# Hash attention and SwiGLU on one core: another order of loads, and two more head pairs turned by TensorE

## The chip, the core and the metric

The kernel runs on one core of one Trainium2 chip. The metric is device time in microseconds of one execution. Three runs of the kernel before gave 378.98, 381.4 and 386.73 us (median 381.4). A separate execution was profiled; it took 378.15 us, and its span from the first to the last instruction is 376.4 us.

## The reference

Four batches, eight heads, 768 tokens, 64 values per head. Every token of q and k gets a bucket of six bits, the signs of its products with a 64 x 6 matrix. A query attends only to keys of its own bucket. The attention output is laid out as 3072 rows of 512 and goes through RMS norm and a SwiGLU network without bias.

```
q_bits = (einsum('bhsd,dk->bhsk', q, proj) > 0);  k_bits likewise
mask   = bucket(q_bits)[..., :, None] == bucket(k_bits)[..., None, :]
scores = where(mask, q @ k^T / 8, -1e9);  attn = softmax(scores);  o = attn @ v
x  = o as [B*S, H*D];  xn = x / sqrt(mean(x*x) + 1e-6) * rms_g
y  = (silu(xn @ w_gate) * (xn @ w_val)) @ w_out        # d_ff = 1536
```

## The kernel before, in words

**Mask by extra rows.** The mask is not applied to the scores. Beside the 64 values, the transposed q and k in tile `QK` have 12 more rows with scaled bits, so that the product q.k over 76 rows (`KROWS`) is pulled far down wherever the bits differ. These rows come from `hash_head` (one head), `hash_heads` (a pair) or `hash_two` (two pairs): products of the transposed fp32 q and k with `proj` on TensorE (`hash_bank`, L202), a comparison on DVE (`signs`, L209), and copies of 12 rows to partitions 64 to 75 of `QK`. [...]

**Turning.** q and k arrive with tokens on partitions and must be transposed. Batch 0 is turned by TensorE per head (`turn_head`, `turn_pe`, L155): three 128 x 128 transposes for k and three for q into a PSUM bank, copied to fp32 tiles `kT` (DVE, L162) and `qT` (ACT, L165), cast to `QK` by ACT and POOL. A bank of PSUM comes from pool `gps`, three in all, which also serves the hash, the gate, value and output products. A `QK` half of a batch 0 head has four blocks of 384 columns: t = 0 even chunks of k, 1 even chunks of q, 2 odd chunks of k, 3 odd chunks of q. Batches 1 to 3 are loaded in blocks of 32 tokens (`load_blocks`: eight DMAs of 96 KB for a pair, 128-byte runs) and turned on DVE by 32 x 32 transposes (`turn_dve`, L186: four instructions for a pair), then cast on POOL (`cast_pool`, L194).

**Units, slots and steps.** A unit is a half batch (384 queries, all 8 heads); the first half of batch 0 is cut in two (units 0 and 1 with 128 and 256 queries). Every head of a unit has one to three slots; a slot is one 128 x 768 tile of scores. There are 192 slots, and the main loop has a step for each: it issues the scores of slot s+1 (L324), the exponential of slot s on ACT (L334), and then everything that `plan[s]` holds, in the order in which `at(s, ...)` was called. Unit 0 has steps 0 to 7, unit 1 steps 8 to 23, each later unit 24 steps from `BASE` (24, 48, 72, ...). `plan` thus is an order written by hand on every engine. It holds: AV products of a head one to three steps later (L348); normalisation (`attn_out`, `norm`); the FFN of the unit before, one gate (L434), one value product (L445) and two DVE operations (L447, L448) at a time; the output products (`project`, L459, from step 23) and their store on SP (L468); loads, turns and hashes of coming heads (table `spots`); and the weight loads.

**Queues.** SP's queue takes loads, bit transfers and stores in the order of the steps; an entry that waits holds up those behind it. POOL issues the weight loads (`load_w` wg and wv in halves at steps 1, 3, 5, 7; `load_wo` at steps 12 and 15), which also cast fp32 to fp16. Raw loads of q, k and v go through pool `lpool` of eight buffers: a new load waits until the tile eight places before it is free. The loads of batch 0 are issued ahead of the loop up to pair 1's v; those of pair 3 at step 1, the last two v at steps 2 and 3.

**Start.** Eight products of zeros (L505, 128 x 512) keep TensorE busy until the first load lands; then heads 0 and 1 are turned, both are hashed, and the scores of slot 0 follow.

Of the kernel before, what the change touches and what calls it, by code (L numbers as in the profile page):

```python
# [36 lines left out]

@with_exitstack
def kernel(
# [16 lines left out]
    lpool = ctx.enter_context(tc.tile_pool(name="lpool", bufs=8))  # L56
# [15 lines left out]
    zeros16 = const.tile([128, 512], FP16, name="zeros16")  # L72
# [20 lines left out]
    def raw_tile(b, hp, which):  # L93
        shape = [128, 24, 32] if b and which != "v" else [128, 2, 6, D]
        raw[b, hp, which] = lpool.tile(shape, FP32, name=which + "L", tag="L")
        return raw[b, hp, which]
# [25 lines left out]

    T0, QK = {}, {}

    def qk_tile(b, hp):
        QK[b, hp] = qkpool.tile([128, 2, 2 * S], FP16, name="QK")
# [6 lines left out]
    def t0(hp, which, hh):  # L133
        return T0[0, hp, which][:, hh * HALF : (hh + 1) * HALF]

    def koff(b, jt):
        return (jt // 3) * S + (jt % 3) * 128 if b == 0 else S + jt * 128

    def qoff(w):
        b, half = divmod(w, 2)  # L140
        return half * S + HALF if b == 0 else half * HALF

    def vchunk(b, jt):
        return 2 * (jt % 3) + jt // 3 if b == 0 else jt

    def turn_pe(h, which):
        hp, hh = divmod(h, 2)
        if (0, hp) not in QK:
            qk_tile(0, hp)
        if hh == 0:  # L150
            t_tile(0, hp, which)
        src = raw[0, hp, which][:, hh].rearrange("p (c e) d -> p c (e d)", e=2)
        ps = bank("t_ps", [128, 3, 128])
        for i in range(3):
            nc.tensor.transpose(ps[:, i, :], src[:, i], ident)  # L155
        return ps.rearrange("p c t -> p (c t)")

    def block(h, t):
        return QK[0, h // 2][0:64, h % 2, t * HALF : (t + 1) * HALF]

    def keep_k(h, ps):
        nc.vector.tensor_copy(t0(h // 2, "k", h % 2), ps)  # L162

    def keep_q(h, ps):
        nc.scalar.copy(t0(h // 2, "q", h % 2), ps)  # L165
        nc.scalar.copy(block(h, 1), ps[0:64])

    def cast_pool0(h, which, par):
        src = t0(h // 2, which, h % 2)[64 * par : 64 * par + 64]
        nc.gpsimd.tensor_copy(block(h, 2 * par + (which == "q")), src)  # L170

    def turn_head(h):
        keep_k(h, turn_pe(h, "k"))
        keep_q(h, turn_pe(h, "q"))
        cast_pool0(h, "k", 0)
        cast_pool0(h, "k", 1)

    def turn_dve(b, hp, which, part):
        if (b, hp) not in QK:
            qk_tile(b, hp)  # L180
# [33 lines left out]
    def bit_rows(h, t):  # L214
        return QK[0, h // 2][D:KROWS, h % 2, t * HALF : (t + 1) * HALF]

    def hash_head(h, q_by_act=False):
        hp, hh = divmod(h, 2)
        kt, qt = t0(hp, "k", hh), t0(hp, "q", hh)
        ps = hash_bank([(pk[:, 0:32], kt), (pq[:, 0:32], qt), (pk[:, 12:44], kt)])  # L220
        bt = spool.tile([128, S], FP16, name="bits")
        signs(bt[:, 0:HALF], ps, 96)
        if q_by_act:
            nc.scalar.copy(bit_rows(h, 1), bt[32:44, 0:HALF])
        nc.vector.tensor_copy(bit_rows(h, 0), bt[0:12, 0:HALF])
        if not q_by_act:
            nc.vector.tensor_copy(bit_rows(h, 1), bt[32:44, 0:HALF])
        nc.vector.tensor_copy(bit_rows(h, 2), bt[64:76, 0:HALF])
        return bt

    def late_bits(h, bt):
        nc.sync.dma_start(out=bit_rows(h, 3), in_=bt[44:56, 0:HALF])

    def hash_heads(hp):
        ps = hash_bank(
            [(w, t0(hp, which, hh)) for hh in range(2) for w, which in ((pk, "k"), (pq, "q"))
             for w in (w[:, 0:32],)]
        )
        bt = spool.tile([128, S], FP16, name="bits")
        signs(bt[:, 0:HALF], ps)  # L240
        for hh in range(2):
            nc.sync.dma_start(
                out=bit_rows(2 * hp + hh, 2), in_=bt[64 * hh + 12 : 64 * hh + 24, 0:HALF]
            )
        for hh in range(2):
            for t in range(2):
                p0 = 64 * hh + 32 * t
                nc.vector.tensor_copy(bit_rows(2 * hp + hh, t), bt[p0 : p0 + 12, 0:HALF])
        for hh in range(2):
            nc.sync.dma_start(  # L250
                out=bit_rows(2 * hp + hh, 3), in_=bt[64 * hh + 44 : 64 * hh + 56, 0:HALF]
            )
# [63 lines left out]
    def scores(g):  # L316
        u, h, p = SLOTS[g]
        w, c0, n = UNITS[u]
        b = w // 2
        t = QK[b, h // 2][0:KROWS, h % 2]  # L320
        ps = scps.tile([128, 2, 512], FP32, name="s_ps")
        for jt, i0, ni, bk, col in score_parts(n, p):
            ko, qo = koff(b, jt), qoff(w) + 128 * c0 + i0
            nc.tensor.matmul(  # L324
                ps[:, bk, col : col + ni], t[:, ko : ko + 128], t[:, qo : qo + ni],
                start=True, stop=True,
            )
        sps[g] = ps
# [9 lines left out]
    def av(u, h, i0, i1):  # L338
        w, c0, n = UNITS[u]
        b = w // 2  # L340
        hp, hh = divmod(h, 2)
        if hh == 0 and i0 == 0:
            ot[u, hp] = ops.tile([128, 3, 2, 66], FP32, name="o_ps")
        o = ot[u, hp]
        for i in range(i0, i1):
            c, jt = divmod(i, 6)
            p, bk, col = prob_at(n, jt, c)
            nc.tensor.matmul(  # L348
                o[:, c, hh, 0:65],
                psb[u, h][:, p, bk, col : col + 128],  # L350
                vls[b % 2][:, h, vchunk(b, jt), 0:65],
                start=(hh == 0 and i == 0), stop=(jt == 5),
                skip_group_check=True,
            )
# [99 lines left out]
    def project(w, c, f0, f1):  # L454
# [8 lines left out]
        if f1 == NF:  # L463
# [4 lines left out]
            nc.sync.dma_start(out=rows[:, 2 * c + half if b == 0 else 3 * half + c, :], in_=ysb)  # L468
# [14 lines left out]
    load_rows(nc.sync, 0, 1, "v")  # L483

    nc.vector.memset(zeros16, 0.0)
# [14 lines left out]
    nc.vector.memset(ones16, 1.0)  # L500
# [3 lines left out]
    for i in range(8):  # L504
        nc.tensor.matmul(wz, zeros16[:, 0:128], zeros16, start=True, stop=True)  # L505
# [27 lines left out]
    turn_head(0)  # L533
    turn_head(1)
    bt0 = hash_head(0, q_by_act=True)
    bt1 = hash_head(1)
# [8 lines left out]
    at(0, late_bits, 0, bt0)  # L545
    at(0, late_bits, 1, bt1)
# [10 lines left out]
    at(3, hash_heads, 3)  # L557
    at(4, v_prep, 0, 2)
    at(1, load_rows, nc.sync, 0, 3, "k")
    at(1, load_rows, nc.sync, 0, 3, "q")  # L560
    at(2, load_rows, nc.sync, 0, 2, "v")
    at(3, load_rows, nc.sync, 0, 3, "v")
    at(5, lambda: nc.sync.dma_start(out=gcol, in_=moe_rms_g.rearrange("(k p) -> p k", p=128)))
    at(6, v_prep, 0, 3)
    for h in range(H):
        at(8 + h, cast_pool0, h, "q", 1)
# [7 lines left out]
    spots = {  # L574
# [3 lines left out]
    }  # L578
    for b, (loads, turns) in spots.items():
        for hp in range(4):  # L580
            s = loads[hp]
            at(s, load_blocks, nc.sync, b, hp)
            at(s, load_rows, nc.sync, b, hp, "v")
            s = turns[hp]
            at(s, turn_dve, b, hp, "k", 0)
            at(s + 1, turn_dve, b, hp, "k", 1)
            at(s + 2, cast_pool, b, hp, "k")
            at(s + 2, turn_dve, b, hp, "q", 0)
            at(s + 3, turn_dve, b, hp, "q", 1)
            at(s + 4, cast_pool, b, hp, "q")  # L590
            if hp % 2:
                at(s + 5, hash_two, b, hp - 1)
            at(s + 5, v_prep, b, hp)
            if b > 1:
                at(s + 5, v_sum, b, hp)
                if hp % 2:
                    at(48 * b + 1 + hp, v_mean, b, hp - 1, 4)
            else:
                at(48 * b + 5 + hp, v_mean, b, hp, 2, range(6))
# [107 lines left out]
```

## Time and profile before

| what | us |
|---|---|
| profiled execution | 378.15 |
| its span | 376.4 |
| median of three runs (lowest, highest) | 381.4 (378.98, 386.73) |
| TensorE busy | 337.9 (90%) |
| DVE, ACT, POOL busy | 238.9, 207.6, 136.6 |
| exponential, L334: 192 of 0.811 | 148.3 |
| DVE transposes, L186: 48 of 0.87 | 41.4 |
| weight loads: time to landing | 7.1 to 11.2 each |

The profile lists for each line of the kernel what ran, how long, and what ended the idle time in front of it. PE is TensorE's products, PEld its weight loads, SPq and POOLq the instructions that issue DMAs. The granted clock of TensorE is given in tenths in the page and as a fraction in the table by stage. `t_ps` are the transposes by TensorE, `d_ps` the hash products, `s_ps` the scores, `o_ps` AV, `g_ps` and `v_ps` gate and value, `y_ps` the output; `kL`, `qL`, `vL` the raw loads.

### The profile page before, as it was taken

The numbers are of one execution on the slowest core, as the hardware profiler recorded it, in microseconds if no ns is written. First come the engines' busy times: TensorE is split into PE (matmuls) and PEld (weight loads), VectorE is DVE, ScalarE is ACT, GpSimd is POOL, SyncE is SP. The second block draws the span as 40 slices with busy tenths as digits, with TensorE's granted clock in tenths as the row PEclk, the third lists the DMA queues.
The fourth block names the chain that finished last, engine by engine and source line by source line (L and its number), as shares of the span: only waits on it lengthen the run. The fifth ranks groups of instructions, "written<-read, shape, count | busy, mean of one in ns | idle before, by whom it ended". The sixth has DMA issues, their size and how long they took to land.

```text
span 376.4 us, 8018 instructions
## 1 busy us (share of the span) xinstructions
PE 337.9 (90%) x3088; PEld 210.2 (56%) x3088; DVE 238.9 (63%) x554; ACT 207.6 (55%) x342; POOL 136.6 (36%) x209
## 2 busy tenths in 40 slices
PE   7627698798979999999999999999999999998995
PEld 3415586476546565565556555656556655664552
DVE  3625256498956895698469846886566636575670
ACT  3414477575635674566656565775566755661331
POOL 4325472066741474286028711773111111111000
PEclk9987689999999999999999999999999999999999
DMA  7273999955074991100589701000100010002002
GB/s 238 101 150 85 215 187 202 170 106 110 14 156 89 151 158 54 73 2 8 91 165 217 128 17 57 29 2 16 57 30 0 2 57 28 2 3 75 12 0 84
DMA packets 91174, 31.42 MB, mean 83 GB/s; under 512 B 77592, under 2 KB 88064, under 8 KB 91136
## 3 DMA queue, kind: packets, MB, share of 16 engines
q1 hardware_dynamic: 87088, 25.80, 31.0%
q0 software_dynamic: 3680, 4.72, 8.0%
q8 instruction: 24, 0.39, 0.5%
q10 hardware_dynamic: 368, 0.39, 0.3%
q14 instruction: 14, 0.11, 0.1%
HBM read 28.32 MB, written 6.29 MB: 92 GB/s over the span
## 4 chain that ended last, share of the span: by engine, by line
PE 73%; DVE 10%; DMA 8%; ACT 3%; issue 2%; SPq 2%; POOL 1%; DVEq 0%; POOLq 0%; ACTq 0%
PE g_ps L434 15%; PE y_ps L459 15%; PE s_ps L324 14%; PE v_ps L445 14%; PE o_ps L348 8%; PE d_ps L202 3%; DMA wo<-in_moe_w_out_dram 3%; DMA qL<-in_q_dram 2%; DMA QK<-bits 2%; DVE xnT L418 2%; DVE kT L186 2%; ACT psb L334 2%; DMA kL<-in_k_dram 1%; DVE bits L209 1%; PE x_ps L417 1%
## 5 line engine op out<-in xcount | busy, mean ns | idle before, releaser
L334 ACT ACTIVATE psb<-s_ps 128x768 f16<-128x768 f32 x192 | 148.3, 811 | 10.7 <-PE s_ps L324 10.6
L324 PE MATMUL s_ps<-QK 76*128 76x384 f16 (+2 forms) x448 | 96.8, 310 | 12.0 <-DMA QK<-bits 4.9
L436 ACT ACTIVATE t<-g_ps 128x384 f32<-128x384 f32 (+2 forms) x108 | 49.2, 456 | 72.0 <-PE g_ps L434 68.8
L445 PE MATMUL v_ps<-xnT,wv 128*128 128x384 f16 (+2 forms) x432 | 80.5, 309 | 3.0 <-DVE a L447 2.8
L434 PE MATMUL g_ps<-xnT,wg 128*128 128x384 f16 (+2 forms) x432 | 80.5, 309 | 1.9 <-DVE xnT L418 1.7
L459 PE MATMUL y_ps<-wo,ht 128*128 128x512 f16 x288 | 70.6, 378 | 1.5 <-DMA wo<-in_moe_w_out_dram 1.5
L447 DVE SCALAR_TENSOR_TENSOR a<-t,g_ps 128x384 f32<-128x384 f32 (+2 forms) x108 | 54.1, 501 | 27.4 <-ACT t L436 26.5
L324 PEld LDWEIGHTS <-QK 76*128 76x128 f16 x448 | 42.5, 101 | 43.6 <-issue 13.8
L348 PEld LDWEIGHTS <-psb 128*128 128x128 f16 x1152 | 53.9, 99 | 18.9 <-issue 3.7
L448 DVE SCALAR_TENSOR_TENSOR ht<-a,v_ps 128x384 f16<-128x384 f32 (+2 forms) x108 | 55.1, 510 | 13.4 <-PE v_ps L445 3.1
L348 PE MATMUL o_ps<-vl,psb 128*128 128x65 f16 x1152 | 59.5, 195 | 0.4 <-ACT psb L334 0.2
L372 POOL TENSOR_TENSOR x<-otmp,rcp 128x384 f32<-128x384 f32 (+2 forms) x27 | 20.4, 756 | 105.1 <-DVE rcp L369 105.0
L445 PEld LDWEIGHTS <-wv 128*128 128x128 f16 x432 | 38.3, 98 | 22.8 <-issue 4.6
L434 PEld LDWEIGHTS <-wg 128*128 128x128 f16 x432 | 38.7, 98 | 21.3 <-issue 2.5
L466 ACT COPY ysb<-y_ps 128x512 f32<-128x512 f32 x24 | 14.1, 586 | 61.0 <-PE y_ps L459 57.8
L459 PEld LDWEIGHTS <-ht 128*128 128x128 f16 x288 | 25.8, 97 | 26.6 <-issue 2.4
L364 DVE TENSOR_TENSOR otmp<-o_ps,cvb 128x390 f32<-128x390 f32 (+2 forms) x36 | 18.5, 513 | 17.3 <-PE o_ps L348 17.2
L194 POOL CAST QK<-qT 64x768 f16<-64x768 f32 x24 | 19.7, 822 | 12.3 <-DVE qT L186 11.5
L418 DVE TENSOR_TENSOR xnT<-x_ps,gcol 128x512 f16<-128x512 f16 x24 | 15.2, 685 | 13.6 <-PE x_ps L417 13.5
L400 POOL TENSOR_SCALAR ms<-ss 128x3 f32<-128x3 f32 (+2 forms) x9 | 1.8, 195 | 56.6 <-DVE ss L398 56.6
L384 POOL TENSOR_TENSOR sq<-x 128x384 f32<-128x384 f32 (+2 forms) x27 | 20.4, 755 | 2.1
L194 POOL CAST QK<-kT 64x768 f16<-64x768 f32 x24 | 19.9, 829 | 3.1 <-DVE kT L186 1.7
(68 smaller groups left out, 261.2 us busy)
## 6 DMA issues: line engine op xcount, KB each, us to landing
vL<-in_v_dram SPq DMA_DIRECT2D x16, 384.0 KB
out_dram<-ysb SPq DMA_DIRECT2D x24, 256.0 KB
qL<-in_q_dram SPq DMA_DIRECT2D x48, 96.0 KB
kL<-in_k_dram SPq DMA_DIRECT2D x48, 96.0 KB
wg<-in_moe_w_gate_dram POOLq DMA_DIRECT2D x2, 768.0 KB, 8.2
wv<-in_moe_w_val_dram POOLq DMA_DIRECT2D x2, 768.0 KB, 7.9
wo<-in_moe_w_out_dram POOLq DMA_DIRECT2D x2, 768.0 KB, 10.4
kL<-in_k_dram SPq DMA_DIRECT2D x3, 384.0 KB
```

Source lines behind the costliest of these rows:

```text
L194: nc.gpsimd.tensor_copy(QK[b, hp][0:64, hh, o : o + S], T0[b, hp, which][64 * hh : 64 * hh + 64, :])
L324: nc.tensor.matmul(ps[:, bk, col : col + ni], t[:, ko : ko + 128], t[:, qo : qo + ni], start=True, stop=True,)
L334: nc.scalar.activation(psb[u, h][:, p], sps.pop(g)[:, :, 0:HALF], AF.Exp, scale=ESCALE,)
L348: nc.tensor.matmul(o[:, c, hh, 0:65], psb[u, h][:, p, bk, col : col + 128], vls[b % 2][:, h, vchunk(b, jt), 0:65], start=(hh == 0 and i == ...
L372: eng.tensor_mul(xd.rearrange("p c (h d) -> p c h d", h=2), tmp[:, 0:n, :, 0:64], r[:, 0:n].to_broadcast([128, n, 2, 64]),)
L418: nc.vector.tensor_mul(xnT[w][:, :, c * 128 : (c + 1) * 128], ps, gcol.unsqueeze(2).to_broadcast([128, 4, 128]),)
L434: nc.tensor.matmul(g, wg[:, kt, fs], xnT[w][:, kt, cs], start=(kt == 0), stop=(kt == 3))
L436: nc.scalar.activation(t, g, AF.Tanh, scale=0.5)
L445: nc.tensor.matmul(vv, wv[:, kt, fs], xnT[w][:, kt, cs], start=(kt == 0), stop=(kt == 3))
L447: nc.vector.scalar_tensor_tensor(out=a, in0=t, scalar=1.0, in1=g, op0=ALU.add, op1=ALU.mult)
L448: nc.vector.scalar_tensor_tensor(out=ht[w][:, ft, cs], in0=a, scalar=0.5, in1=vv, op0=ALU.mult, op1=ALU.mult)
L459: nc.tensor.matmul(y, ht[w][:, ft, c * 128 : (c + 1) * 128], wo[:, ft, :], start=(ft == 0), stop=(ft == NF - 1),)
```

## The change

- **Start.** The warm-up has 28 products of 128 columns in place of eight of 512, with ones in place of zeros. Head 0 is hashed before head 1 is turned. In `hash_head` ACT always copies the q bits.
- **Loads of batch 0.** `lpool` has ten buffers. Pair 1's v, then pair 3's k and q are issued at step 0 right behind pair 1's first bit transfers; the last two v at step 1. The bits of block 3 (odd q, used only from the second half of the batch on) leave `hash_heads`; `late_bits` sends them on SP at steps 3 and 5 to 7.
- **Batch 1, pairs 0 and 1** are in `BY_PE`: loaded in rows (three DMAs of 384 KB a pair, at steps 8 and 12), turned by TensorE, a head's k or q per step at steps 10 to 13 and 16 to 19, copied by DVE (k) and ACT (q), cast on POOL in two halves a step later, and hashed a pair at a time at steps 14 and 20, with all four bit blocks by DMA on SP. `k_cols`, `q_cols`, `v_chunk` and `out_chunk` hold the layouts of chunks; batch 1 now stores even and odd chunks, and for its pairs 2 and 3, still turned by DVE, the score's queries are read with a stride between chunks.
- **Other turns.** The four transposes of a pair stand two steps apart, in table `work`, where before all four stood in consecutive steps. Loads, hash and v of a pair move with them: loads eight steps before the turn (nine in two cases), the v one step after q and k, hash and v preparation two steps after the last transpose. `load_wo` is at steps 9 and 11.

The core of the diff:

```diff
-    lpool = ctx.enter_context(tc.tile_pool(name="lpool", bufs=8))
+    lpool = ctx.enter_context(tc.tile_pool(name="lpool", bufs=10))
+BY_PE = [(0, hp) for hp in range(4)] + [(1, 0), (1, 1)]
...
+    def q_cols(w, h, i0, ni):
...
+        if b == 1:
+            return t[:, 0:S].rearrange("p (c e t) -> p e c t", e=2, t=128)[:, half]
...
+    def keep(eng, b, h, which):
+        ps = turn_pe(b, h, which)
+        (eng.copy if eng is nc.scalar else eng.tensor_copy)(t0(b, h, which), ps)
+        return ps
...
+    def hash_heads(b, hp):
+        ps = hash_bank(
+            [(w[:, 0:32], t0(b, 2 * hp + hh, which))
+             for hh in range(2) for w, which in ((pk, "k"), (pq, "q"))]
+        )
+        bt = bits_tile(hp + 1 if b == 0 else hp)
+        signs(bt, ps)
         for hh in range(2):
+            h, p0 = 2 * hp + hh, 64 * hh
+            nc.sync.dma_start(out=bit_rows(b, h, 2), in_=bt[p0 + 12 : p0 + 24])
+            if b == 0:
+                for t in range(2):
+                    nc.vector.tensor_copy(bit_rows(b, h, t), bt[p0 + 32 * t : p0 + 32 * t + 12])
+                late[h] = bt[p0 + 44 : p0 + 56]
+            else:
+                for t in range(2):
+                    nc.sync.dma_start(
+                        out=bit_rows(b, h, t), in_=bt[p0 + 32 * t : p0 + 32 * t + 12]
+                    )
+                nc.sync.dma_start(out=bit_rows(b, h, 3), in_=bt[p0 + 44 : p0 + 56])
...
-    load_rows(nc.sync, 0, 1, "v")
...
-    for i in range(8):
-        nc.tensor.matmul(wz, zeros16[:, 0:128], zeros16, start=True, stop=True)
+    for i in range(28):
+        nc.tensor.matmul(wz[:, 0:128], ones16, ones16, start=True, stop=True)
...
     turn_head(0)
+    hash_head(0)
     turn_head(1)
-    bt0 = hash_head(0, q_by_act=True)
-    bt1 = hash_head(1)
+    hash_head(1)
     scores(0)
...
-    at(0, hash_heads, 1)
+    at(0, hash_heads, 0, 1)
+    at(0, load_rows, nc.sync, 0, 1, "v")
+    at(0, load_rows, nc.sync, 0, 3, "k")
+    at(0, load_rows, nc.sync, 0, 3, "q")
     at(0, turn_head, 4)
     at(1, turn_head, 5)
-    at(1, hash_heads, 2)
+    at(1, hash_heads, 0, 2)
+    at(1, load_rows, nc.sync, 0, 2, "v")
+    at(1, load_rows, nc.sync, 0, 3, "v")
...
+    at(3, late_bits, 0)
+    at(3, late_bits, 1)
...
-    at(1, load_rows, nc.sync, 0, 3, "k")
-    at(1, load_rows, nc.sync, 0, 3, "q")
-    at(2, load_rows, nc.sync, 0, 2, "v")
-    at(3, load_rows, nc.sync, 0, 3, "v")
+    for h in range(2, H):
+        at(4 + h // 2, late_bits, h)
...
-        at(12 + 3 * i, load_wo, 6 * i, 6 * i + 6)
-
-    spots = {
-        1: ((16, 20, 33, 38), (32, 37, 43, 48)),
-        2: ((52, 56, 63, 68), (61, 67, 80, 86)),
-        3: ((96, 100, 106, 112), (104, 110, 128, 134)),
+        at(9 + 2 * i, load_wo, 6 * i, 6 * i + 6)
+    work = {
+        (1, 0): (8, (10, 11, 12, 13)), (1, 1): (12, (16, 17, 18, 19)),
+        (1, 2): (25, (33, 35, 37, 39)), (1, 3): (33, (41, 43, 45, 47)),
+        (2, 0): (50, (58, 60, 62, 64)), (2, 1): (58, (66, 68, 70, 72)),
+        (2, 2): (74, (82, 84, 86, 88)), (2, 3): (81, (89, 91, 93, 95)),
+        (3, 0): (97, (105, 107, 109, 111)), (3, 1): (105, (113, 115, 117, 119)),
+        (3, 2): (121, (130, 132, 134, 136)), (3, 3): (129, (137, 139, 141, 143)),
     }
+    for (b, hp), (s, turns) in work.items():
+        done = turns[3] + 2
+        if (b, hp) in BY_PE:
+            at(s, load_rows, nc.sync, b, hp, "k")
+            at(s, load_rows, nc.sync, b, hp, "q")
+            at(s + 1, load_rows, nc.sync, b, hp, "v")
+            for i, s in enumerate(turns):
+                h, which = 2 * hp + i // 2, "kq"[i % 2]
+                at(s, keep, nc.scalar if i % 2 else nc.vector, b, h, which)
+                for par in range(2):
+                    at(s + 1, cast_half, b, h, which, par)
+            at(turns[3] + 1, hash_heads, b, hp)
```

More of the change, by code (lines that the diff above doesn't have):

```diff
@@ L93, in raw_tile @@
     def raw_tile(b, hp, which):
-        shape = [128, 24, 32] if b and which != "v" else [128, 2, 6, D]
+        shape = [128, 24, 32] if which != "v" and (b, hp) not in BY_PE else [128, 2, 6, D]
         raw[b, hp, which] = lpool.tile(shape, FP32, name=which + "L", tag="L")
@@ L125, in qk_tile @@
     def qk_tile(b, hp):
-        QK[b, hp] = qkpool.tile([128, 2, 2 * S], FP16, name="QK")
+        if (b, hp) not in QK:
+            QK[b, hp] = qkpool.tile([128, 2, 2 * S], FP16, name="QK")
     def t_tile(b, hp, which):
@@ L212, in signs @@
         )
[L214 to L219, printed above, removed]
-        ps = hash_bank([(pk[:, 0:32], kt), (pq[:, 0:32], qt), (pk[:, 12:44], kt)])
[L221 to L229, printed above, removed]
@@ L231, in late_bits, with bit_rows, bits_tile, hash_head @@
-    def late_bits(h, bt):
-        nc.sync.dma_start(out=bit_rows(h, 3), in_=bt[44:56, 0:HALF])
-    def hash_heads(hp):
+    def bit_rows(b, h, t):
+        return QK[b, h // 2][D:KROWS, h % 2, t * HALF : (t + 1) * HALF]
+    late = {}
+    held = []
+    def bits_tile(i):
+        if i % 2 == 0:
+            held.append(spool.tile([128, S], FP16, name="bits"))
+        return held[-1][:, (i % 2) * HALF : (i % 2 + 1) * HALF]
+    def hash_head(h):
+        kt, qt = t0(0, h, "k"), t0(0, h, "q")
+        ps = hash_bank([(pk[:, 0:32], kt), (pq[:, 0:32], qt), (pk[:, 12:44], kt)])
+        bt = bits_tile(h)
+        signs(bt, ps, 96)
+        nc.scalar.copy(bit_rows(0, h, 1), bt[32:44])
+        nc.vector.tensor_copy(bit_rows(0, h, 0), bt[0:12])
+        nc.vector.tensor_copy(bit_rows(0, h, 2), bt[64:76])
+        late[h] = bt[44:56]
@@ L235, in hash_heads, with late_bits @@
+    def late_bits(h):
+        nc.sync.dma_start(out=bit_rows(0, h, 3), in_=late[h])
+    def hash_heads(b, hp):
         ps = hash_bank(
-            [(w, t0(hp, which, hh)) for hh in range(2) for w, which in ((pk, "k"), (pq, "q"))
-             for w in (w[:, 0:32],)]
-        )
-        bt = spool.tile([128, S], FP16, name="bits")
-        signs(bt[:, 0:HALF], ps)
+            [(w[:, 0:32], t0(b, 2 * hp + hh, which))
+             for hh in range(2) for w, which in ((pk, "k"), (pq, "q"))]
+        )
+        bt = bits_tile(hp + 1 if b == 0 else hp)
+        signs(bt, ps)
@@ L241, in hash_heads @@
         for hh in range(2):
[L242 to L252, printed above, removed]
+            h, p0 = 2 * hp + hh, 64 * hh
@@ L467, in project @@
             rows = out[b * S : (b + 1) * S, :].rearrange("(p c) n -> p c n", c=6)
-            nc.sync.dma_start(out=rows[:, 2 * c + half if b == 0 else 3 * half + c, :], in_=ysb)
+            nc.sync.dma_start(out=rows[:, out_chunk(w, c), :], in_=ysb)
             del obank[w, c]
@@ L571 @@
         at(s1, load_w, wv, moe_w_val, 768 * i, 768 * i + 768)
-        at(12 + 3 * i, load_wo, 6 * i, 6 * i + 6)
-    spots = {
[3 rows of a table removed]
-    }
-    for b, (loads, turns) in spots.items():
-        for hp in range(4):
-            s = loads[hp]
-            at(s, load_blocks, nc.sync, b, hp)
[L583 to L590, printed above, removed]
-            if hp % 2:
[L592 to L599, printed above, removed]
+        at(9 + 2 * i, load_wo, 6 * i, 6 * i + 6)
+    work = {
[6 rows of a table added]
+    }
+    for (b, hp), (s, turns) in work.items():
[10 more added lines that the diff above has]
+            at(turns[3] + 1, hash_heads, b, hp)
+        else:
+            at(s, load_blocks, nc.sync, b, hp)
+            at(s + 1, load_rows, nc.sync, b, hp, "v")
+            for i, s in enumerate(turns):
+                at(s, turn_dve, b, hp, "kq"[i // 2], i % 2)
+                if i % 2:
+                    at(s + 1, cast_pool, b, hp, "kq"[i // 2])
+            if hp % 2:
+                at(done, hash_two, b, hp - 1)
+        at(done, v_prep, b, hp)
+        if b == 1:
+            at(48 + 2 * hp, v_mean, b, hp, 2, range(6))
+        else:
+            at(done, v_sum, b, hp)
+            if hp % 2:
+                at(48 * b + 1 + hp, v_mean, b, hp - 1, 4)
     gts, sqs = {}, {}
```

76 lines of the change are left out of this document (36 added, 40 removed).

## The prediction

> **What bounds the kernel now.** I read the page first, then busy time by stage, then what TensorE waited for up to 62 us, then the order of time on TensorE, SP and POOL around those waits.
>
> ```profile
> span 376.4 us, 8018 instructions
> PE 337.9 (90%) x3088; PEld 210.2 (56%) x3088; DVE 238.9 (63%) x554; ACT 207.6 (55%) x342; POOL 136.6 (36%) x209
> PEclk9987689999999999999999999999999999999999
> ```
>
> TensorE is busy 90% of the span, so 38.5 us are idle, and the clock falls only at the start. The table by stage (PE, PEld, DVE, ACT, POOL busy, granted clock, DMA share, GB/s) says where:
>
> ```profile
> 10.00:20.00 10.00, 7.21 (x58) 4.48 (x58) 5.82 (x14) 5.31 (x12) 4.52 (x9) 1.00 0.21 75
> 20.00:30.00 10.00, 2.17 (x20) 1.38 (x18) 2.09 (x6) 0.53 (x1) 1.27 (x2) 0.78 0.86 200
> 30.00:40.00 10.00, 5.88 (x62) 4.38 (x60) 4.61 (x14) 3.92 (x7) 6.80 (x12) 0.84 0.45 66
> 40.00:50.00 10.00, 8.41 (x95) 7.46 (x96) 3.98 (x14) 6.21 (x8) 5.45 (x11) 0.67 1.20 210
> ...
> 62.20:98.20 36.00, 30.05 (x335) 21.10 (x334) 26.51 (x62) 23.30 (x40) 15.59 (x21) 1.00 0.66 125
> 98.20:142.15 43.95, 40.82 (x388) 24.23 (x385) 34.09 (x71) 25.46 (x40) 23.50 (x31) 1.00 0.71 124
> 142.15:182.00 39.85, 39.05 (x353) 23.12 (x354) 29.07 (x61) 23.58 (x38) 20.18 (x28) 1.00 0.09 28
> ```
>
> From 20 to 50 us TensorE works 16.5 us of 30, part of it at half clock. From 142 us it is busy 39.05 of 39.85 us for 24 steps: there only less TensorE work saves time. Between, 62 to 142 us, 9 us are idle. The waits up to 62 us, and the lines around them (start, length, in brackets the idle time before):
>
> ```profile
> PE t_ps L155 <- DMA kL<-in_k_dram: 8.8, 2, 7.7
> PE s_ps L324 <- DMA QK<-bits: 4.9, 2, 4.1
> ```
>
> ```profile
> 17.95 0.33 PE L324 MATMUL s_ps<-QK 76*128 76x128 f16 x3 [0.83 <-DMA QK<-bits]
> 20.46 0.50 PE L324 MATMUL s_ps<-QK 76*128 76x128 f16 x6
> 28.62 0.87 PE L155 MATMUL t_ps<-ident,kL 128*128 128x128 f32 x3 [7.65 <-DMA kL<-in_k_dram]
> 31.33 0.83 PE L324 MATMUL s_ps<-QK 76*128 76x128 f16 x6
> 40.66 0.50 PE L324 MATMUL s_ps<-QK 76*128 76x128 f16 x3 [4.08 <-DMA QK<-bits]
> ```
>
> ```profile
> 15.97 1.48 SPq L242 DMA_DIRECT2D QK<-bits  x2
> 21.08 1.48 SPq L242 DMA_DIRECT2D QK<-bits  x2
> 24.19 0.46 SPq L106 DMA_DIRECT2D kL<-in_k_dram  x1
> 35.13 1.53 SPq L242 DMA_DIRECT2D QK<-bits  x2
> ```
>
> ```profile
> 20.26 1.01 POOL L522 DMA_DIRECT2D wg<-in_moe_w_gate_dram  x1
> 34.32 0.80 POOL L522 DMA_DIRECT2D wv<-in_moe_w_val_dram  x1
> ```
>
> The reader is to see two things. Pair 3's k is issued at 24.19, behind all bit transfers of pairs 1 and 2, and TensorE stands for it until 28.62. And a 9 KB transfer of bits takes 15.97 to 17.95 = 1.98 us when no weights are moving, but 35.13 to 40.66 = 5.53 us when a weight load went out 0.8 us before it. Pair 2's bits (21.08) also follow a weight load (20.26) by 0.8 us; the long wait for k hides what they took.
>
> **The change part by part.** The sum is against the profiled execution: 378.15 us, span 376.4 and 1.75 around it. It lies 0.9% under the median of the runs shown (381.4).
>
> Unit 0, loads in order of use. In the new order pair 3's k and q and pair 1's v are issued right after pair 1's two bit transfers: about 17, 17.5 and 18 us, and land by about 22 (before, k took 24.19 to 28.62 with a weight load moving). The 7.65 us go. Late next are pair 2's bits: scores of head 4, at 31.33 before, need them. The first head's hash now stands ahead of the second head's turn, which waited for a load until 6.75; I take 0.5 us for that (bounds 0 and 1.0), so they are issued at 20.6. POOL's weight load moves with them. At 5.53 us they land at 26.1: a gain of 31.33 - 26.1 = 5.2 us. Bounds: 5.53 us is the slow row; with 1.98 us TensorE has its k and q at 22 to 23 and the gain is 8.3 us. I take the slow row, because the order of weight load and bits is the same as at 34.32 and 35.13. The late q bits (two, then six, 0.72 us each on SP) now stand ahead of the loads of batch 1, which are issued early anyway.
>
> Pair 3's bits still follow the wv load by 0.8 us: the wait of 4.08 stays. 0, bounds -4.1 and 0.
>
> Rows instead of blocks for batch 1's pairs 0 and 1. TensorE now waits for k of pair (1,0) at step 10 and q at step 11; before, DVE took them at 32. SP issues them about 35 to 36 us (behind the late bits, each of which waits for a transfer eight places earlier), while weight loads follow one another. Step 11 would be at about 41.4 (46.8 before, less 5.2 and the half clock). A 384 KB load took 4.8 us from issue next to a weight load (qL, 24.75 to 29.6); two in a row under three more weight loads land between 40 and 48, so the wait is between 0 and 5, I take +2.5. Behind the waiting transpose stand scores, AV and gate of unit 1.
>
> TensorE's added work: 24 transposes in 8 groups of 3. At full clock a group takes 0.35 (t_ps starts at 12.12, 12.46 and 12.79), at half clock 0.87. 8 x 0.35 = +2.8, and it is on the path, since from 50 to 62 us TensorE is busy 11.94 of 12. The hash of these pairs moves from step 42 to 14 and 20: 16 records in 1.43 us both ways, +1.4 here and -1.4 below.
>
> Hidden parts: DVE loses 8 transposes of 0.87 (-7.0) and gains 4 copies of 0.56; ACT gains 4 copies of 0.48; POOL swaps 8 casts of 0.82 for 16 of 0.50 (+1.4) and issues wo sooner. From 44.5 to 62.2 ACT is busy 13.3 of 17.7, DVE 10.6, POOL 9.8, so about 4 us more on POOL and 2 on ACT fit; without that cover POOL's casts would cost up to 8 us. SP swaps 16 block loads for 4, and 8 bit transfers for 16 of 0.72; they end before pair (1,2) is needed. The warm-up goes from 8 products of 512 columns (0.43 each) to 28 of 128: 0, bounds -0.6 and +1 for a colder start.
>
> Clock: at half from 25.6 to 32.4, 39.2 to 46 and 49.4 to 52.9. The idle time before the first shrinks from 7.65 to about 3, the second stays, step 11 adds one: -1.0, bounds -4 and +2.
>
> wo at steps 9 and 11 instead of 12 and 15: y_ps waited 1.47 at 66.47 and scores behind it 0.88 for ACT. Take -2.0, bounds -2.4 and 0 (if the weight queue is still busy).
>
> Steps 31 to 48: the hash that left is -1.4; v_ps waited 2.2 for DVE in 62 to 98, where DVE had 12 transposes in its queue and now has 8: -1.2. Together -2.6, bounds -1.4 and -3.6.
>
> Steps 48 to 72 took 43.95 against 39.85 for the next 24. They have 3 y_ps groups less (-2.6), four v_mean (+1.3) and a second hash (+1.4): at the later density 40.0, so 4 us are lost, around the last turn of pair (1,3) (hash waits 1.2 for it) and the crowded DVE. All of (1,3) is turned by 47 now: -3.5, bounds 0 and -4.
>
> Other turns: loads of (2,2), (3,0) and (3,2) now stand on SP behind eight bit transfers (6.27) with 8 to 9 steps to the turn. Hash start 2.2, bits 6.3, q 2.8, k 2.7, landing 1.5: some 16 us; from step 74 to 82 it is 12.8 + 1.4 for the hash, and DVE lags about 1.4: 15.6. +0.7 in all, bounds 0 and 3 us in each of five places.
>
> Sum: -5.2 + 2.5 + 2.8 + 1.4 - 1.0 - 2.0 - 2.6 - 3.5 + 0.7 = -6.9, so 378.15 - 6.9 = 371.2 us. Its own range is 367 to 376.
>
> On the held transfers, the Trainium skill, "DMA: Bandwidth & Descriptors", section "Queues, rings and completion order", says that each DMA engine takes its queue rows in turn, a packet at a time. By that rule small transfers would hardly be held by a weight load; the trace (5.53 against 1.98 us) speaks against it here, and the sum goes by the trace.
>
> **The rivals.**
>
> Small transfers are not held: pair 2's bits land in about 2 us, since what was slow at 35.13 was something else, or the new order gets them ahead of the weights. Then 3.1 more in unit 0, most of the 4.08 wait (3.6) and the 2.5 at step 11 go: 371.2 - 9.2 = 362.0. For it: bits sent at 15.97 took 1.98. Against: 40.66 above. It is what the rule of the skill just named would give.
>
> Batch 1's loads come late and cold: 5 us at step 11, 1.5 at step 17 for q of (1,1), and half clock through steps 10 to 17 (2.0 more than summed): 371.2 + 2.5 + 1.5 + 2.0 = 377.2, about no change. For it: DMA share 1.20 from 40 to 50 us. Against: these loads have 1536-byte rows, and 768 such packets went in 24.19 to 29.6. The skill's "TensorE: Matmul & The Clock Gate", section "Part 4: PE-mode transpose", says that transposes don't count as busy for the clock; that would help this rival. From 12 to 20 us the clock stayed at 1.00 with transposes and hash products, which speaks against it.
>
> Slower: the loads behind bit transfers. In five places (steps 33, 58, 82, 105, 130) DVE's transpose waits for kL, and behind it in DVE's queue stand the a and ht products of the FFN, and so v_ps and g_ps on TensorE. At 3 us each: 371.2 - 0.7 + 15 = 385.5. It decides from 1.5 us each (7.6 / 5 places). Against: the margins worked out above are near 0 and not -3.
>
> **How the numbers follow.** Forecast 0.46, not held 0.27, late and cold 0.16, loads behind bits 0.08, anything else 0.03. The predicted time is the first case's, 371.2. The range 361 to 379 takes in the second case nearly whole and the third; outside are the fourth and some of the second's lower part, under 0.2. 2% of 378.15 is 7.6 us, about what a measurement can tell from no change: the line is 370.6, which splits the forecast case in half. Faster: 0.23 + 0.27 = 0.50. Same: 0.23 + 0.16 + 0.01 = 0.40. Slower: 0.08 + 0.02 = 0.10.
>
> **What would show it.** In the new profile: no wait of t_ps for kL above 2 us near 21; a wait of s_ps for bits near 23 to 26 (head 4) and another of about 4 us for head 6; a wait of t_ps for kL or qL at step 10 or 11; no wait for wo; 24 steps from 48 on in about 40 us instead of 43.95; DVE transposes with little idle time before them. The prediction is wrong if head 4's bits are not waited for, if batch 1's turns stall more than 5 us, or if DVE stands for kL late in the run.

## The result and the profile after

The changed kernel takes 393.42 us (median of 4 runs, 392.44 to 395.9) against 380.5 us for the kernel before beside it: a ratio of 1.036 [1.029, 1.044]. It is slower; the prediction was 371.2, with a range of 361 to 379. The profiled execution took 395.9 us, its span is 394.1.

Lines have moved: scores are now L342 (324 before), the exponential L352 (334), the transposes L170 (155), the value product's `a` L465 (447), the copy of the output into `ysb` L484 (466), its store L486 (468), block loads L119 (117), the bit transfers of two pairs L287 (267). From the page of the kernel after, size, busy time and granted clock:

```profile
span 394.1 us, 8094 instructions
PE 348.3 (88%) x3132; PEld 216.6 (55%) x3132; DVE 235.8 (60%) x548; ACT 209.9 (53%) x347; POOL 137.7 (35%) x217
PEclk9986679999999999899988999789999999999999
```

TensorE is busy 10.4 us more than before, though it has only 44 products more. The clock line says why: behind the start, where before it was 9 all through, it now falls in three more places, the first near 160 us. The table by stage of the kernel after shows the start first, then stretches between the same steps (step 23 at 68.31, 48 at 100.09, 72 at 139.73, 96, 120, 144 and 168; from step 48 on the mark is the first output product, `y_ps`, of the step; columns as before):

```profile
20.00:30.00 10.00, 6.07 (x56) 4.14 (x55) 3.71 (x11) 3.11 (x6) 4.54 (x8) 0.84 0.95 238
30.00:40.00 10.00, 5.39 (x53) 3.26 (x52) 2.94 (x10) 3.05 (x5) 4.94 (x8) 0.67 0.84 137
40.00:50.00 10.00, 7.06 (x66) 6.11 (x65) 3.98 (x14) 4.38 (x8) 6.69 (x13) 0.67 1.11 259
68.31:100.09 31.78, 28.93 (x328) 21.14 (x326) 23.70 (x58) 24.03 (x41) 12.79 (x17) 1.00 0.46 86
100.09:139.73 39.64, 37.55 (x361) 22.92 (x359) 28.82 (x63) 23.75 (x39) 16.03 (x21) 1.00 0.39 78
139.73:183.53 43.80, 40.44 (x354) 23.61 (x352) 29.36 (x61) 24.54 (x40) 18.62 (x25) 0.96 0.37 77
183.53:230.54 47.01, 42.08 (x356) 24.39 (x354) 29.42 (x62) 24.44 (x40) 17.99 (x25) 0.93 0.34 71
230.54:278.13 47.59, 42.07 (x354) 24.27 (x353) 28.83 (x60) 24.43 (x40) 17.89 (x25) 0.93 0.35 71
278.13:318.12 39.99, 39.07 (x355) 23.29 (x354) 24.10 (x54) 24.45 (x40) 9.68 (x14) 1.00 0.07 24
```

The loss lies in three stretches of 24 steps: 43.80, 47.01 and 47.59 us, where the kernel before took 39.73, 39.83 and 39.66. (The last row is 1.5 above its 38.46 for another reason: one more hash lies between step 72 and 168, since each was moved by some steps; in the kernel before it stands just ahead of the mark of step 72.) The same number of products (354 to 356) keeps TensorE busy 40.4 to 42.1 us there and 39.07 in the stretch without a loss. So a stall costs its wait and then slow products behind it.

Who stalls? What ScalarE and TensorE waited for in the kernel after (total, times, longest):

```profile
ACT ysb L484 <- DMA out_dram<-ysb: 15.7, 2, 8.1
```

```profile
PE s_ps L342 <- ACT psb L352: 13.1, 14, 4.7
PE s_ps L342 <- DMA QK<-bits: 11.5, 3, 4.6
PE t_ps L170 <- DMA kL<-in_k_dram: 2.6, 1, 2.6
```

The first line is not in the kernel before at all: ScalarE waits twice, about 8 us each, for a store. The order of time on SP, then ScalarE, then TensorE around the first of them:

```profile
187.95 6.59 SPq L287 DMA_DIRECT2D QK<-bits  x8
194.64 2.71 SPq L119 DMA_DIRECT2D qL<-in_q_dram  x4
197.39 2.71 SPq L119 DMA_DIRECT2D kL<-in_k_dram  x4
200.20 0.58 SPq L486 DMA_DIRECT2D out_dram<-ysb  x1
```

```profile
188.47 0.58 ACT L484 COPY ysb<-y_ps 128x512 f32<-128x512 f32 x1 [3.90 <-PE y_ps L477]
192.84 0.58 ACT L484 COPY ysb<-y_ps 128x512 f32<-128x512 f32 x1 [1.64 <-PE y_ps L477]
193.32 2.22 ACT L352 ACTIVATE psb<-s_ps 128x768 f16<-128x768 f32 x3
203.09 0.58 ACT L484 COPY ysb<-y_ps 128x512 f32<-128x512 f32 x1 [7.55 <-DMA out_dram<-ysb]
203.57 0.82 ACT L352 ACTIVATE psb<-s_ps 128x768 f16<-128x768 f32 x1
```

```profile
199.50 0.81 PE L463 MATMUL v_ps<-xnT,wv 128*128 128x384 f16 x4
204.44 0.80 PE L342 MATMUL s_ps<-QK 76*128 76x384 f16 x2 [4.12 <-ACT psb L352]
205.03 1.48 PE L452 MATMUL g_ps<-xnT,wg 128*128 128x384 f16 x4
...
211.82 0.81 PE L452 MATMUL g_ps<-xnT,wg 128*128 128x384 f16 x4
```

Read them from the top. The output buffer filled at 188.47 is to be stored by SP, but eight bit transfers and eight block loads stand ahead on SP; the store goes out at 200.20, some 11 us after its copy. `ysb` has two buffers. The second is filled at 192.84, and the third copy needs the first, so it starts at 203.09, 2.9 us after the store was issued. The next exponential stands behind that copy on ScalarE and starts at 203.57, and TensorE, which needs its score bank back, stands 4.12 us. It comes back at half clock: the same four gate products take 1.48 us at 205.03 and 0.81 at 211.82. Around 248 us it happens again, with 8.13 us on ScalarE.

In the kernel before, the hash of the same two pairs came at step 91 and not 97. On SP:

```profile
175.15 6.16 SPq L267 DMA_DIRECT2D QK<-bits  x8
187.60 0.40 SPq L468 DMA_DIRECT2D out_dram<-ysb  x1
```

The bits were out by 181.31, the loads behind them by 187.50, and the store followed 1.8 us after its copy had ended (185.81).

The third loss is another thing. On DVE, and on TensorE behind it:

```profile
160.89 0.86 DVE L200 STREAM_TRANSPOSE kT<-kL 128x384 f32<-128x384 f32 x1 [3.51 <-DMA kL<-in_k_dram]
```

```profile
162.19 1.04 PE L463 MATMUL v_ps<-xnT,wv 128*128 128x384 f16 x4 [2.46 <-DVE a L465]
```

This is step 82, where the transpose of pair (2,2) waits for k, whose loads stand behind eight bit transfers; `a` and the value product queue behind it.

At the start, the scores of unit 0 wait for bits three times. On TensorE and on SP, the kernel after:

```profile
19.51 0.48 PE L342 MATMUL s_ps<-QK 76*128 76x128 f16 x3 [2.92 <-DMA QK<-bits]
29.02 0.33 PE L342 MATMUL s_ps<-QK 76*128 76x128 f16 x3 [3.94 <-DMA QK<-bits]
38.71 0.50 PE L342 MATMUL s_ps<-QK 76*128 76x128 f16 x3 [4.61 <-DMA QK<-bits]
47.30 0.90 PE L170 MATMUL t_ps<-ident,kL 128*128 128x128 f32 x3 [2.56 <-DMA kL<-in_k_dram]
```

```profile
15.44 1.66 SPq L262 DMA_DIRECT2D QK<-bits  x2
18.70 0.46 SPq L108 DMA_DIRECT2D kL<-in_k_dram  x1
23.81 1.53 SPq L262 DMA_DIRECT2D QK<-bits  x2
33.16 1.48 SPq L262 DMA_DIRECT2D QK<-bits  x2
```

Pair 3's k goes out at 18.70 instead of 24.19 and the 7.65 us wait for it is gone, but bits take its place: from issue to the scores that use them 5.2 us for head 4 and 5.5 for head 6. Those scores of head 6 start at 38.71, 1.95 us sooner than before.

### The profile page after: what moved, and what is told of

The parts are those of the page before. It is cut to its first block, busy times and chain, and to the rows that moved or that the text cites. A ratio compares the mean times of both kernels' runs of the same rounds, so it can differ in the third digit from the quotient of the medians.

```text
span 394.1 us, 8094 instructions
## 1 busy us (share of the span) xinstructions
PE 348.3 (88%) x3132; PEld 216.6 (55%) x3132; DVE 235.8 (60%) x548; ACT 209.9 (53%) x347; POOL 137.7 (35%) x217
## 4 chain that ended last, share of the span: by engine, by line
PE 72%; DMA 8%; DVE 6%; SPq 6%; ACT 4%; issue 2%; POOL 0%; DVEq 0%; ACTq 0%
PE g_ps L452 16%; PE s_ps L342 14%; PE v_ps L463 14%; PE y_ps L477 13%; PE o_ps L366 8%; PE d_ps L216 4%; SPq L119 4%; DMA QK<-bits 4%; DMA kL<-in_k_dram 3%; ACT psb L352 3%; SPq L287 2%; PE t_ps L170 2%; DVE xnT L436 2%; DMA out_dram<-ysb 1%; DVE bits L223 1%
## 5 line engine op out<-in xcount | busy, mean ns | idle before, releaser
L352 ACT ACTIVATE psb<-s_ps 128x768 f16<-128x768 f32 x192 | 148.5, 812 | 11.6 <-PE s_ps L342 11.6
L342 PE MATMUL s_ps<-QK 76*128 76x384 f16 (+2 forms) x448 | 99.3, 316 | 26.7 <-ACT psb L352 13.1
L452 PE MATMUL g_ps<-xnT,wg 128*128 128x384 f16 (+2 forms) x432 | 83.5, 317 | 2.9 <-DVE xnT L436 2.3
L463 PE MATMUL v_ps<-xnT,wv 128*128 128x384 f16 (+2 forms) x432 | 82.2, 314 | 2.8 <-DVE a L465 2.8
L465 DVE SCALAR_TENSOR_TENSOR a<-t,g_ps 128x384 f32<-128x384 f32 (+2 forms) x108 | 54.4, 504 | 39.6 <-ACT t L454 37.7
L342 PEld LDWEIGHTS <-QK 76*128 76x128 f16 x448 | 43.0, 102 | 60.3 <-issue 22.9
L484 ACT COPY ysb<-y_ps 128x512 f32<-128x512 f32 x24 | 14.0, 585 | 70.3 <-PE y_ps L477 54.7
L208 POOL CAST QK<-kT 64x768 f16<-64x768 f32 x20 | 16.4, 820 | 37.9 <-DVE kT L200 20.4
L223 DVE TENSOR_SCALAR bits<-d_ps,thr,scl 128x384 f16<-128x384 f32 (+1 forms) x17 | 11.3, 677 | 22.7 <-PE d_ps L216 22.7
L208 POOL CAST QK<-qT 64x768 f16<-64x768 f32 x20 | 16.4, 820 | 14.0 <-DVE qT L200 13.3
```

The lines of the kernel that those rows point to most:

```text
L208: nc.gpsimd.tensor_copy(QK[b, hp][0:64, hh, o : o + S], T0[b, hp, which][64 * hh : 64 * hh + 64, :])
L342: nc.tensor.matmul(ps[:, bk, col : col + ni], k_cols(b, h, jt), q_cols(w, h, 128 * c0 + i0, ni), start=True, stop=True,)
L352: nc.scalar.activation(psb[u, h][:, p], sps.pop(g)[:, :, 0:HALF], AF.Exp, scale=ESCALE,)
L452: nc.tensor.matmul(g, wg[:, kt, fs], xnT[w][:, kt, cs], start=(kt == 0), stop=(kt == 3))
L463: nc.tensor.matmul(vv, wv[:, kt, fs], xnT[w][:, kt, cs], start=(kt == 0), stop=(kt == 3))
L465: nc.vector.scalar_tensor_tensor(out=a, in0=t, scalar=1.0, in1=g, op0=ALU.add, op1=ALU.mult)
```

## The experiments

Theory: the loss is the stores, which stand on SP behind loads and bit transfers since loads of batches 2 and 3 moved to the steps where a hash and the output products are; a smaller part is the k of step 82. Rivals: the turning by TensorE or the start costs it; or the late loads themselves do, through DVE. A second question is what holds the bits at the start. In the first set the kernel before measured 378.9 us (19 runs), in the second 379.85 (13), in the last 380.68 (6).

**Four output buffers** (`e1_ysb4`). Two more `ysb`; `lpool` gives one up for room.

```diff
-            ysb = spool.tile([128, DMODEL], FP32, name="ysb")
+            ysb = spool.tile([128, DMODEL], FP32, name="ysb", bufs=4)
```

> The changed kernel with four ysb buffers in place of two (and nine raw buffers in place of ten, to make room). Theory (stores): in two places ACT stands 7.6 and 8.1 us for a free ysb buffer, because the store that would free it waits on SP behind eight bit transfers and eight block loads; TensorE then loses about 5.7 and 6.4 us. With four buffers both waits go: 394 - 12 = about 382 us; the 2.6 us that TensorE loses to the kL wait near 160 us stay. Rival (loads): the loads behind the bits are late for DVE whatever the stores do; then DVE stands for kL at the same two places instead and the time stays within 3 us of 393.

Measured: 378.18 us, 0.999 [0.995, 1.003] of before. About 14 us go (from 1.036 of before to 0.999), and ScalarE waits for no store any more. What DVE then waits for:

```profile
DVE kT L200 <- DMA kL<-in_k_dram: 7.0, 4, 3.9
```

Freed of the stores, the loads are somewhat more in the way, in four places. From step 72 to 168 this kernel takes 164.48 us (137.72 to 302.20), the changed one 178.39, the one before 157.68: the stores cost 13.9 us of the 20.7. The time is 4 us below the 382 expected, which counted 12 us for the two stalls.

**Three loads eight steps earlier** (`e2_loads_early`). They no longer follow a hash in the same step.

```diff
-        (2, 2): (74, (82, 84, 86, 88)), (2, 3): (81, (89, 91, 93, 95)),
-        (3, 0): (97, (105, 107, 109, 111)), (3, 1): (105, (113, 115, 117, 119)),
-        (3, 2): (121, (130, 132, 134, 136)), (3, 3): (129, (137, 139, 141, 143)),
+        (2, 2): (66, (82, 84, 86, 88)), (2, 3): (81, (89, 91, 93, 95)),
+        (3, 0): (89, (105, 107, 109, 111)), (3, 1): (105, (113, 115, 117, 119)),
+        (3, 2): (113, (130, 132, 134, 136)), (3, 3): (129, (137, 139, 141, 143)),
```

> The changed kernel with the loads of pairs (2,2), (3,0) and (3,2) issued eight steps sooner (66, 89, 113), so that they stand on SP ahead of the eight bit transfers and the stores. Theory (queue order on SP is the cause of both kinds of wait): the two ACT waits for ysb shrink to under 1 us each and the kL wait of DVE goes: 394 - 14.7 = 379 us. Rival (bits alone fill SP): the stores still wait 6.3 us behind the bits, half of the loss stays: 386 us.

Measured: 374.38 us, 0.989 [0.984, 0.994]. Steps 72 to 168 take 159.53 us (135.43 to 294.96), and of the 1.85 us that they are above before, 1.5 are the hash that now lies in this stretch. The 379 expected was too high: it counted 14.7 us for the stalls, and the three stretches had lost 19.2. SP around the same place:

```profile
179.55 6.54 SPq L287 DMA_DIRECT2D QK<-bits  x8
186.19 4.83 SPq L486 DMA_DIRECT2D out_dram<-ysb  x3
191.11 2.74 SPq L119 DMA_DIRECT2D qL<-in_q_dram  x4
```

The stores now stand ahead of the loads, behind the bits alone. So 5.0 us more (164.48 - 159.53, with the stores already out of the way) were the loads behind bit transfers, the prediction's last rival; both losses have one cause in the code, three entries of a table.

**The late turns alone** (`e3_late_turns_only`): the kernel before, with the new table for batches 2 and 3 and nothing else.

```diff
+    work = {
+        (2, 0): (50, (58, 60, 62, 64)), (2, 1): (58, (66, 68, 70, 72)),
+        (2, 2): (74, (82, 84, 86, 88)), (2, 3): (81, (89, 91, 93, 95)),
+        (3, 0): (97, (105, 107, 109, 111)), (3, 1): (105, (113, 115, 117, 119)),
+        (3, 2): (121, (130, 132, 134, 136)), (3, 3): (129, (137, 139, 141, 143)),
+    }
```

> The kernel before with only the new steps for loads, turns, hash and v of batches 2 and 3. Theory: this part alone brings the stalls near 160, 200 and 248 us, about 14 us: 379 + 14 = 393 us. Rival (the first 70 us are what costs): within 4 us of 379.

Measured: 393.04 us, 1.039 [1.032, 1.046]. This part alone makes the whole loss, 14 us, and the rivals that put it on the start or on TensorE's turning are out. ScalarE stands for a store twice here too:

```profile
ACT ysb L466 <- DMA out_dram<-ysb: 16.3, 2, 8.6
```

**The start alone** (`e4_start_only`): the changed kernel up to the end of batch 0's loads and hashes; `BY_PE` holds batch 0 only, `load_wo` and the old table `spots` are as before.

```diff
-BY_PE = [(0, hp) for hp in range(4)] + [(1, 0), (1, 1)]
+BY_PE = [(0, hp) for hp in range(4)]
```

> The kernel before with only the new start: warm-up, ten raw buffers, order of batch 0's loads, late q bits, hash of head 0 ahead. Batch 1, wo and all later turns at the old steps. By the changed kernel's trace, scores of head 6 came 2.0 us sooner (38.7 against 40.7): 377 us, a gain of about 2. By the prediction: a gain of 5 to 6, 373. Rival (the early part costs): 381 or more.

Measured: 373.5 us, 0.988 [0.984, 0.992]: the start is worth 5.4 us, as the prediction had it and not 2, as the changed kernel's trace suggested. The version with early loads (374.38) has all the rest of the change too and is no better, so two pairs turned by TensorE, spread turns and an earlier wo together are worth about nothing.

**Weights out of the bits' way** (`e5_weights_late`), from the version with early loads.

```diff
-    for i, (s0, s1) in enumerate(((1, 3), (5, 7))):
+    for i, (s0, s1) in enumerate(((5, 6), (7, 8))):
```

> The version with the loads of (2,2), (3,0) and (3,2) eight steps earlier (374.4 us), with wg and wv loaded two to four steps later, so that no weight load goes out next to a bit transfer of batch 0. If bit transfers are held by a weight load in flight (5.2 us from issue to the scores that use them, 2 us alone), the waits of scores for bits of heads 4 and 6 (3.9 and 4.6 us in the changed kernel) fall to under 1 us each and 4 to 6 us go from the time, less a wait of the gate for weights of up to 2 us: 369 to 372. The rival, that each transfer gets its turn and the bits are late for another reason (their hash and issue), leaves both waits at about 4 us and the time at 374 or above.

Measured: 377.67 us, 0.995 [0.991, 0.999], so 2 to 3 us slower than its base (0.989 of the kernel before beside it) instead of 2 to 5 faster. The scores of head 6 on TensorE and the issue of their bits on SP, in the base:

```profile
36.45 0.50 PE L342 MATMUL s_ps<-QK 76*128 76x128 f16 x3 [4.05 <-DMA QK<-bits]
```

```profile
31.03 1.48 SPq L262 DMA_DIRECT2D QK<-bits  x2
```

And in this version, with what TensorE waits for next:

```profile
30.35 0.34 PE L342 MATMUL s_ps<-QK 76*128 76x128 f16 x3 [0.95 <-DMA QK<-bits]
43.31 0.90 PE L170 MATMUL t_ps<-ident,kL 128*128 128x128 f32 x3 [7.50 <-DMA kL<-in_k_dram]
```

```profile
28.46 1.48 SPq L262 DMA_DIRECT2D QK<-bits  x2
```

The mechanism was right: without a weight load beside them (the first goes out at 31.49) the bits of head 6 take 28.46 to 30.35 = 1.9 us, where in the base they took 31.03 to 36.45 = 5.4. The time was not: the weights now meet batch 1's rows, and the wait that leaves the bits turns up as 7.50 us at step 10.

**No bit transfers in batch 0** (`e6_no_bit_dma`), from the version with early loads and the old weight steps: each head is hashed alone, with a third product that puts the bits of block 2 at rows 64 to 75, from where DVE copies them. The bits get four buffers, `lpool` nine.

```diff
-    at(0, hash_heads, 0, 1)
+    at(0, hash_head, 2)
+    at(0, hash_head, 3)
```

and likewise for pairs 2 and 3.

> The same version (374.4 us) with every head of batch 0 hashed so that its bits reach Q and K by copies of VectorE, with no transfer for the second block. If the bits' transfers are what unit 0 waits for, no scores of unit 0 wait for a DMA any more; 2.9 + 3.9 + 4.6 us of waits become some 3 us of extra hash, copies and their latency: 367 to 371. The rival, that the transfers only hid a lack of other operands (loads of k and q, the hash itself), leaves 373 to 376.

Measured: 368.78 us, 0.972 [0.967, 0.978], as expected: no scores of unit 0 wait for a DMA, and about 6 us go (from 0.989 of before to 0.972). The waits for bits were a loss of this start and could be had.

**Rows of batch 1 sooner** (`e7_rows_sooner`), from the last one.

```diff
-    for h in range(2, H):
-        at(4 + h // 2, late_bits, h)
+    for h in range(H):
+        at(8 + h // 2, late_bits, h)
...
-            at(s, load_rows, nc.sync, b, hp, "k")
-            at(s, load_rows, nc.sync, b, hp, "q")
+            at(3 + 2 * hp, load_rows, nc.sync, b, hp, "k")
+            at(3 + 2 * hp, load_rows, nc.sync, b, hp, "q")
```

> As the version without bit transfers, and the row loads of batch 1's pairs 0 and 1 issued at steps 3 and 5, with all late bits behind them. If the wait of the turn at step 10 for k (2.56 us in the changed kernel) is the place of the loads on SP, it goes, and the time is 1.5 to 3 us below the version without bit transfers: 365 to 369. If the loads share their bandwidth with the weights, the wait moves to another operand (bits of the late heads, wg or wv) and the time stays within 1 us of that version.

Measured: 364.73 us, 0.962 [0.957, 0.966]: 4 us below its base, and no transpose of TensorE waits for a load. The loads' place on SP set the wait: k went out at 28.30 in the base, behind all late bits, and at 13.53 here. Whether weight loads beside them also delayed the rows is not shown: all four loads of k and q now go out by 18.70, and the first weight load at 20.25. This is the best version, 7% below the changed kernel.

**The same start, turned by DVE** (`e8_start_no_bit_dma`): the start alone, with the hash per head as above; spread turns and the earlier wo are left out too.

> The start of the changed kernel without bit transfers, and from batch 1 on all turns by VectorE at the places of the kernel before (373.5 us with bit transfers). Against the version without bit transfers that turns two pairs of batch 1 by TensorE it tells what that turning is worth. By the terms of the prediction it is worth rows' wait +2.5, transposes +2.8, hash moved 0, steps 31 to 72 about -6: about 0, so this kernel comes out within 1.5 us of the other. A rival: TensorE's turning only costs where the start is not late, and this kernel is faster by 2 us or more.

Measured: 365.03 us, 0.963 [0.958, 0.968]. It is 3.7 us faster than its partner with TensorE's turning and late rows (368.78), which is what the rival said, and within 0.3 us of the one with rows sooner. So turning two pairs by TensorE, with the spread turns and the earlier wo, costs where its rows are late and is worth nothing measurable where they are not. It moves the time: this kernel's first scores of step 23 start at 50.25 and those of the version with rows sooner at 54.88, which then takes 3.6 us less to step 48.

**Stores issued by ScalarE** (`e9_store_act`), from the changed kernel, still two output buffers.

```diff
-            nc.sync.dma_start(out=rows[:, out_chunk(w, c), :], in_=ysb)
+            nc.scalar.dma_start(out=rows[:, out_chunk(w, c), :], in_=ysb)
```

> The changed kernel with its output stores issued by ScalarE itself, right behind the copy that fills the buffer, instead of by SP; buffers, loads and bit transfers unchanged. If the loss came from stores that stood on SP behind loads and bit transfers, ScalarE waits for no store any more, the waits of scores for ScalarE late in the run (4.1 and 4.7 us) go, and the time comes to that of the kernel with four output buffers, 376 to 381, at the price of 48 issues on ScalarE that should be hidden. The rival, that the loads and bit transfers themselves are late (DVE waits for k in four places, 7.0 us in all with four buffers), leaves 388 to 394.

Measured: 385.54 us, 1.011 [1.001, 1.021]: 8 us better than the changed kernel, and between the two ranges. What ScalarE waited for:

```profile
ACT psb L352 <- ACT ysb L484: 7.6, 18, 0.4
ACT ysb L484 <- DMA out_dram<-ysb: 4.0, 2, 2.0
```

The waits of 7.6 and 8.1 us shrink to two of 2.0, so the place on SP was their cause. But the issue is not hidden: each store takes ScalarE 0.34 us and 0.42 us of standing between the copy and the next exponential, and a stretch of 24 steps that was 39.99 us is now 41.23 (266.28 to 307.51). There are 24 stores, three in such a stretch, and not the 48 issues of the expectation.

## Why the prediction was wrong

The prediction's terms by stretch of the profiled executions, without the 1.75 us around the span:

| stretch | predicted | measured |
|---|---|---|
| to the scores of head 6 (40.66 before) | -5.2 | -1.95 |
| from there to step 23 (+2.5 + 2.8 + 1.4 - 1.0) | +5.7 | +8.08 |
| steps 23 to 48 (wo -2.0, -2.6) | -4.6 | -4.56 |
| steps 48 to 72 | -3.5 | -3.92 |
| step 72 to the end | +0.7 | +20.05 |
| sum | -6.9 | +17.7 |

**The step that failed** is "Other turns: loads of (2,2), (3,0) and (3,2) now stand on SP behind eight bit transfers ... +0.7 in all, bounds 0 and 3 us in each of five places". It saw the right eight entries of SP's queue and asked one question of them: is k there when DVE turns it? The stores of the output stand on the same queue behind the same loads, and nobody was asked about those. The kernel after shows them as 15.7 us on ScalarE; more buffers alone take about 14 us off the time. DVE's own waits, which the term priced, were 4.4 us in two places, and the loads behind bit transfers cost about 5 (first two experiments). Here the term was too small: at step 82 the last block of k had gone out by 157.46 and the transpose began at 160.89, 3.4 us later, where the term took 1.5 for the landing. The term should have read about +19: 13.9 for stores and 5.0 for loads; the rest of the 20.05 is mostly the hash that crossed step 72. Even its upper bound, 15 in five places, was for another mechanism; what cost time were two places at 7 to 8 us each and one at 4 (43.80 - 39.73).

A stall was also priced at its wait alone. At 204.44 TensorE waited 4.12 us and the stretch lost 7.2 (47.01 - 39.83): 3.0 of these are the same products at half clock (42.08 busy against 39.07).

**The first term, -5.2, was half right.** Pair 3's load wait went and bits were late next: 5.2 us from issue to use for head 4, beside a weight load, as forecast (with the weights moved away, head 6's take 1.9 us instead of 5.4). But they were issued at 23.81 and not 20.6. One reason is the 2.92 us wait for pair 1's bits at 19.51 in this execution, 4.07 us after their issue. In four other profiles with the same start that wait is 0.95 to 0.97, pair 2's bits go out between 20.71 and 22.04, and the scores of head 6 come between 36.45 and 38.92. The one at 38.92 had no long wait either, so how much of the miss belongs to this execution, none or up to 2.3 us, is open. Why these bits took longer in it is not settled: an instruction load (a 16 KB packet of queue q8) moved at the same time on the DMA engines, but one also moved near these bits in the version with the start alone and in the one with weights late, where the wait is 0.97 and 0.96.

**The second stretch**, +8.08 for +5.7: the wait at step 10 was forecast at 2.5 and is 2.56. TensorE's busy time grew by 5.15 us (20.54 to 25.69) for 40 more products, at a mean clock of 0.80 and 0.81. The prediction priced them at full clock, +4.2, and counted 1.0 for a better clock, which did not come.

**Right** were wo (no wait for it), steps 23 to 48, and within 1 us steps 48 to 72 (-3.92, of which 1.4 is the hash that crossed step 72).

**The rivals.** "Not held" is out for the kernel after (5.2 us), although a version that sends no bits did reach 368.78 with early loads. On this point, the Trainium skill, "DMA: Bandwidth & Descriptors", section "Queues, rings and completion order", has each DMA engine switch between queues packet by packet; 1.9 us against 5.4 for the bits of head 6, with the weights' steps as the only difference, speaks against small transfers being spared, as the prediction had it. "Late and cold" came near the sum up to step 72, -1.6 against -2.35, but by luck: the wait of batch 1 was 2.56 us and not its 5, and what was lost beside that were the bits of unit 0. "Slower: loads behind bit transfers", at 0.08, had the place; its mechanism made about 5 us of the 19.

## What to carry to other kernels

When a load moves on a queue, list everything that stands behind it there, stores above all, and ask of each entry who waits for the buffer that it frees; the distance from a load to its own use is only the first of these questions. Price a stall on a kernel like this one above its wait, for the half clock that follows: waits of 2.46, 4.12 and 4.71 us on TensorE went with stretches that lost 4.07, 7.18 and 7.93 us, about 1.7 times as much. And moving the weights away from the bits passed the wait on to the next loads; sending no bits was what helped here.

## What the runs showed of the hardware

A gap of 2.46 us on TensorE was enough to halve the granted clock. Around the stall at step 82 in the kernel after (159.73 to 162.19), in stretches of 2 us:

```profile
159.00:161.00 2.00, 0.73 (x12) 0.50 (x11) 0.11 (x1) 1.83 (x3) 0.00 (x0) 1.00 0.88 207
161.00:163.00 2.00, 0.81 (x4) 0.43 (x4) 1.90 (x4) 0.06 (x1) 0.00 (x0) 0.91 1.03 308
163.00:165.00 2.00, 2.00 (x8) 0.94 (x7) 1.58 (x3) 0.00 (x0) 0.19 (x1) 0.50 0.96 145
165.00:167.00 2.00, 2.00 (x18) 1.19 (x17) 1.19 (x3) 1.19 (x2) 1.45 (x2) 0.74 0.73 115
```

The clock was still 1.00 in the first part of the gap and was 0.50 for some 3 us when TensorE was at work again; with the 4.12 us gap half clock began before TensorE was back (204.44) and lasted from about 203.6 to 210.4. The length of a gap doesn't settle it alone: in the version with the start alone, a gap of 2.16 us before 61.63 was followed by 1.00 until 66. The Trainium skill, "TensorE: Matmul & The Clock Gate", section "Why this matters for your kernels", warns of idle gaps above about 3 us; here 2.46 us were enough.
